# A fused attention and two-layer MoE kernel: the front and the first nine units written out in another order

## The chip, the cores and the metric

One core of one Trainium2 chip runs the whole kernel in one launch. The metric is the device time of a launch in microseconds (us). Engines are named as in the profile: PE (TensorE; PEld its weight loads), DVE (VectorE), ACT (ScalarE), POOL (GpSimd), SP (SyncE, which here only issues DMAs). Each engine runs its instructions in order.

## What is computed

Linear attention with decay over 12 blocks of 64 positions (2 batches, 8 heads, head size 64), then a two-layer MLP on the 1,536 x 512 result, then a second MLP with a softmax gate and a layer norm. Cut to what matters here:

```python
for b in range(12):                                  # blocks of 64 positions, all heads
    intra = einsum('bhic,bhjc->bhij', qb, kb) * Dmask # scores, masked with powers of lam
    intra = einsum('bhij,bhjd->bhid', intra, vb)
    inter = einsum('bhid,bhde->bhie', qb * lam_pow, kv_state)
    out[b] = intra + inter
    kv_state = lam_block * kv_state + einsum('bhsd,bhse->bhde', kb * rev_pow, vb)
h = x @ w_in                                         # 512 -> 2048
x = maximum(0.01 * h, h) @ w_out                     # 2048 -> 512
h = x @ w_in2                                        # 512 -> 1024; then solu, layer norm with g_ln
out = ln(h) @ w_out2                                 # 1024 -> 512
```

## The kernel before

**Attention** is cut into 12 steps, one for each block of 64 positions. A step has four groups of small 64x64 products on PE: scores (`scores_mm`, L196), their product with v (`xs_mm`, L242), the state's increment (`state_mm`, L210) and q times the state (`xq_mm`, L254). Around them stand: the mask on the scores (`scores_ev`, DVE L204), the decay of k (`scale_k`, four ACT instructions of a head pair each, L170), of q (`scale_q`) and of the state (`decay_state`, both on POOL), the new state (`state_ev`, DVE L236) and the split of the result into two float32r words, `x_hi` (ACT L289) and `x_lo` (DVE L293). Steps 0 to 3 stand in front and give the first 512 tokens (block 0); the other eight stand among the units below (`step`, at the units that `step_at` names).

**The first MLP** runs over 3 blocks of 512 tokens and 16 slices of 128 hidden columns: 48 units (b, f). A unit has a first product (`l1_mm`, L422: 12 matmuls 128x512, in three groups of four: hi word of the weight by hi word of x, hi by lo, lo by hi), the leaky ReLU and the split of its result (`l1_split`: ACT L425, ACT L428, DVE L429) and a second product (`l2_mm`, L438: 12 matmuls) which accumulates in four PSUM banks. The loop runs the first product of unit i, then the second one of unit i-1.

**Weights** arrive as int64 pairs of float32 words in pairs of halves: pair n holds w_in slice n ("IN") and w_out slice n-1 ("OUT"), 512 KB each. Unit (0, f) reads pair f's IN half and pair f+1's OUT half. Each half is converted by ACT and DVE in turn: `words` (two ACT passes, L336 over the high word and L337 over the low one), `clamp`, `shift`, `join` (DVE L343, L353, L362), `high` (ACT L392) and `low` (DVE L411). Block 0 needs all of this done unit by unit; later blocks reuse the result.

**What sets the order.** The code is written out by hand, and its last loop ties every instruction of an engine to the one before it, so each engine runs in the order of the code. All loads go through one helper on one queue (SP), which also limits the bytes under way: a load waits for the landing of the load with which it would pass 1.5 MiB.

```python
AHEAD = 3 << 19
    for before, n in reversed(flight):
        ahead += n
        if ahead > AHEAD:
            tc.add_manual_dep(ins, before.name, SYNC, reason="bytes under way")
```

The order of the loads before: tables (132 KB), step 0 (2 x 384 KB of q, k, k and 256 KB of v), pair 0's IN half, step 1, two DMAs of 64 KB that turn the first mask table `dfirst` into `dmask`, steps 2 and 3, pairs 1 to 3, qk and kv of step 4, pair 4, qk of step 5 and so on. kv has one buffer, qk two.

Of the kernel before, what the change touches and what calls it, by code (L numbers as in the profile page):

```python
# [19 lines left out]
NB = 2  # L20
# [4 lines left out]
AHEAD = 3 << 19  # L25
# [19 lines left out]
def fused_kernel(ctx: ExitStack, tc: tile.TileContext, att, vt, tab, cst, w_in, w_out, w_in2, w_out2, out):  # L45
# [23 lines left out]
    dfirst = cp.tile([P, NPAIR, CH], F32, name="dfirst")  # L69
# [18 lines left out]
    def jrows(s, h):  # L88

        return HALF[h] if s < NPRE else HALF[1 - h]  # L90

    def decay(s):

        return dfirst if s < NPRE else dmask

# [17 lines left out]
    def load(queue, out, in_):  # L113

        size = 4
        for n in out.shape:
            size *= n
        ins = queue.dma_start(out=out, in_=in_).ins
        ahead = size
        for before, n in reversed(flight):  # L120
            ahead += n
            if ahead > AHEAD:
                tc.add_manual_dep(ins, before.name, SYNC, reason="bytes under way")
                break
        flight.append((ins, size))

    def load_step(s):

        t = wp.tile([P, 2048], F32, tag="w", name="ldw")
        qkk = t[:, 0:1536].rearrange("p (n c a b) -> p n c a b", n=NB, c=3, a=NPAIR)  # L130
        v = t[:, 1536:2048].rearrange("p (n a b) -> p n a b", n=NB, a=NPAIR)
        for b in range(NB):
            load(act if s + b == 1 and s == 0 else sync, out=qkk[:, b], in_=att[2 * s + b])
        load(sync, out=v, in_=vt[s])
        ld[s] = (qkk[:, :, 0], qkk[:, :, 1], qkk[:, :, 2], v)

# [22 lines left out]
    def scale_q(s, eng):  # L159
# [3 lines left out]
        q = qk_t[s][:, :, 0] if s >= NPRE else ld[s][Q]  # L163
# [3 lines left out]
    def by_pair(out_, in_, factors):  # L167

        for pr in range(NPAIR):
            act.activation(out_[:, :, pr], in_[:, :, pr], AF.Copy, scale=factors[:, pr, CH - 1 : CH])  # L170

    def scale_k(s, eng):
# [3 lines left out]
        kj, last = ld[s][KJ], decay(s)  # L176
        if eng is act:
            by_pair(kj, kj, last)
# [3 lines left out]
    def decay_state(s, eng):  # L182
# [4 lines left out]
        if eng is act:  # L187
            by_pair(sd_t[s], s_t[s], qpow)
        else:
            eng.tensor_tensor(sd_t[s], s_t[s], qpow[:, :, CH - 1 : CH].unsqueeze(1).to_broadcast(SHAPE), op=ALU.mult)  # L190

    def scores_mm(s, bank, b, pr):
        q, k = (qk_t[s][:, :, 0], qk_t[s][:, :, 1]) if s >= NPRE else ld[s][0:2]
        for h in range(2):
            d = rows(h)
            pe.matmul(at(bank, jrows(s, h), b, pr), k[d, b, pr], q[d, b, pr], start=True, stop=True)  # L196

    def scores_ev(s, bank):
# [15 lines left out]
    def state_ev(s, bank):
# [7 lines left out]
        if s not in sd_t:  # L222
            src = bank.rearrange("p (n a b) -> p n a b", n=NB, a=NPAIR)
            for pr in range(NPAIR):
                ins = dve.scalar_tensor_tensor(
# [6 lines left out]
                ).ins  # L232
                added.setdefault(s, ins)
            return
        for src, dst, old in parts(bank, s_t[s + 1], sd_t[s]):
            added[s] = dve.tensor_tensor(dst, src, old, op=ALU.add).ins  # L236

    def xs_mm(s, bank, b, pr):

        for h in range(2):  # L240
            j = jrows(s, h)
# [64 lines left out]
    def load_weights(n, halves=None):  # L306
# [109 lines left out]
    def l1_mm(u, bank):  # L416
# [15 lines left out]
    def l2_mm(u):
        b, f = u
        ghi, glo = gt.pop(u)
        w = wout_t[f].rearrange("p s (m c) -> p s m c", m=KD)
        for s, g, first, last in ((0, ghi, True, False), (1, ghi, False, False), (0, glo, False, True)):
            for m in range(KD):
                pe.matmul(acc[m], w[:, s, m], g, start=(f == 0 and first), stop=(f == NF - 1 and last))  # L438
# [126 lines left out]
    def scan(table, side, first):  # L565

        for pr in range(NPAIR):
# [6 lines left out]
    load(sync, out=tabs, in_=tab)  # L574
    scan(dfirst, 0, None)
    load_step(0)
    load_weights(0)
    load_step(1)
    for h in range(2):
        load(sync, out=dmask[rows(h)], in_=dfirst[HALF[h]])  # L580
    load_step(2)
    load_step(3)
    load_weights(1, IN)
    load_weights(1, OUT)
    load_weights(2)
    load_weights(3)
    load_qk(NPRE)
    load_kv(NPRE)
    load_weights(4)
    load_qk(NPRE + 1)  # L590
    load(sync, out=fix, in_=cst)
    act.mul(nhalf, one, -0.5)


    xb, sb, kb = acc[0:2], acc[2:4], aps[1]
    alone(scores_mm, 0, sb[0])
    scale_k(0, dve)
    scores_ev(0, sb[0])
    scan(qpow, 1, 1.0)
    scale_q(1, pool)  # L600
    words(0)
    both(xs_mm, 0, xb[0], state_mm, 0, kb)
    state_ev(0, kb)
    x_hi(0, xb[0])
    scale_k(1, act)
    decay_state(1, pool)

    alone(scores_mm, 1, sb[1])
    bits(0)
    scores_ev(1, sb[1])  # L610
    x_lo(0, xb[0])
    both(xs_mm, 1, xb[1], state_mm, 1, kb)
    scale_q(2, pool)
    scale_k(2, act)
    alone(scores_mm, 2, sb[0])
    state_ev(1, kb)
    decay_state(2, pool)
    alone(xq_mm, 1, xb[1])
    scores_ev(2, sb[0])
    join(0)  # L620
    x_hi(1, xb[1])
    both(xs_mm, 2, xb[0], state_mm, 2, kb)
    x_lo(1, xb[1])
    scale_q(3, pool)
    scale_k(3, act)
    high(0)

    alone(scores_mm, 3, sb[1])
    state_ev(2, kb)
# [197 lines left out]
```

## Time and profile before

| | us |
|---|---|
| median of 3 runs (448.31 to 450.56) | 448.86 |
| the profiled execution | 449.68 |
| its span on the core | 447.9 |
| PE busy | 434.0 |
| DVE busy | 266.5 |
| ACT busy | 194.9 |
| mean granted PE clock | 0.992 |

The span is what the profiler sees between the first and the last instruction; the execution's own time is 1.8 us longer, and 0.8 us above the median. Busy times are unions of an engine's instructions; a matmul's end is modelled, and its record (390 ns) is longer than its share of the array (227 ns, 12 in 2.72 us), so an idle PE shows a little too small.

### The profile page before, as it was taken

To read this page: it belongs to the slowest core of one execution; us is meant where nothing else is said; L and a number is where in the kernel's file an instruction comes from. 1 tells how busy PE (TensorE), PEld (TensorE's weight loads), DVE (VectorE), ACT (ScalarE), POOL (GpSimd) and SP (SyncE) were. 2 spreads that over 40 slices of the span, in tenths; PEclk is the share of its full clock that TensorE was granted. 3 is DMA by queue.
4 is the path that set the end of the run, shared out by engine and by line. 5 is a ranking of instruction groups with operands and counts; after the bars stand their busy time and mean duration, and the time that the engine had idled before them with its cause. 6 is when DMAs were issued, how large, how long until landed. Compare 5 with 4: busy or idle time off the path is not lost.

```text
span 447.9 us, 7951 instructions
## 1 busy us (share of the span) xinstructions
PE 434.0 (97%) x3252; PEld 358.2 (80%) x3252; DVE 266.5 (60%) x411; ACT 194.9 (44%) x326; POOL 33.0 (7%) x39
## 2 busy tenths in 40 slices
PE   6879899999999999999999999999999999999996
PEld 3868688888788888888888888888888888888886
DVE  3479898998932121211131788817779877777640
ACT  3477977868443232121233678622423322222221
POOL 0502022020102020100000000000000000000000
PEclk9699999999999999999999999999999999999999
DMA  7888875951303030100015653000112322222111
GB/s 264 253 282 265 288 273 153 320 194 50 94 0 97 1 95 1 48 0 1 1 23 184 225 198 122 1 0 5 44 34 58 98 72 74 74 75 74 58 48 47
DMA packets 23859, 46.98 MB, mean 105 GB/s; under 512 B 4368, under 2 KB 12176, under 8 KB 23312
## 3 DMA queue, kind: packets, MB, share of 16 engines
q1 hardware_dynamic: 21952, 44.92, 30.4%
q10 hardware_dynamic: 1872, 1.58, 1.2%
q8 instruction: 25, 0.41, 0.4%
q14 instruction: 10, 0.08, 0.1%
HBM read 37.95 MB, written 3.15 MB: 92 GB/s over the span
## 4 chain that ended last, share of the span: by engine, by line
PE 84%; DMA 8%; ACT 3%; DVE 2%; issue 1%; SPq 1%; ACTq 0%
PE acc L438 25%; PE hps L422 25%; PE acc L550 15%; PE aps L458 6%; PE hps L458 5%; PE acc L458 4%; DMA ldw<-in_att_dram 3%; DMA raww<-in_w_out_dram 2%; PE aps L242 1%; DMA qk<-in_att_dram 1%; PE aps L254 1%; PE acc L560 1%; DMA raww<-in_w_in_dram 1%; DMA kv<-in_vt_dram 1%; ACT x L336 1%; ACT raww L337 1%
## 5 line engine op out<-in xcount | busy, mean ns | idle before, releaser
L422 PE MATMUL hps<-xhi,wio 128*128 128x512 f32 x384 | 102.9, 390 | 3.1 <-ACT wio L392 2.4
L429 DVE TENSOR_TENSOR glo<-hps,ghi 128x512 fp32r<-128x512 f32 x48 | 33.2, 691 | 116.2 <-ACT ghi L428 115.8
L438 PE MATMUL acc<-ghi,wio 128*128 128x512 f32 x384 | 96.2, 393 | 0.1
L422 PEld LDWEIGHTS hps<-xhi,wio 128*128 128x128 f32 x384 | 71.7, 188 | 19.1 <-ACT wio L392 3.4
L438 PEld LDWEIGHTS acc<-ghi,wio 128*128 128x128 f32 x384 | 71.3, 188 | 15.6 <-ACT ghi L428 0.5
L425 ACT ACTIVATE hps<-hps 128x512 f32<-128x512 f32 x48 | 28.0, 583 | 116.6 <-PE hps L422 116.6
L550 PE MATMUL acc<-wb,ln 128*128 128x512 f32 (+1 forms) x312 | 67.6, 373 | 0.0
L550 PEld LDWEIGHTS acc<-wb,ln 128*128 128x128 f32 x312 | 55.3, 188 | 10.2
L422 PE MATMUL hps<-xlo,wio 128*128 128x512 f32 x192 | 51.4, 389 | 0.0
L438 PE MATMUL acc<-glo,wio 128*128 128x512 f32 x192 | 51.3, 389 | 0.0
L422 PEld LDWEIGHTS hps<-xlo,wio 128*128 128x128 f32 x192 | 36.0, 188 | 7.6
L438 PEld LDWEIGHTS acc<-glo,wio 128*128 128x128 f32 x192 | 36.0, 188 | 7.5
L353 DVE SCALAR_TENSOR_TENSOR raww<-x,raww 128x1024 uint32<-128x1024 uint32 (+1 forms) x27 | 31.2, 1154 | 0.5
L336 ACT ACTIVATE x<-raww 128x1024 f32<-128x1024 f32 (+1 forms) x27 | 27.7, 1027 | 7.5 <-DMA raww<-in_w_in_dram 5.2
L362 DVE SCALAR_TENSOR_TENSOR x<-x,raww 128x1024 uint32<-128x1024 uint32 (+1 forms) x27 | 29.6, 1096 | 0.8
L428 ACT CAST ghi<-hps 128x512 fp32r<-128x512 f32 x48 | 28.2, 587 | 1.5
L337 ACT ACTIVATE raww<-raww 128x1024 uint32<-128x1024 uint16 (+1 forms) x27 | 27.9, 1033 | 0.0
L491 POOL TENSOR_TENSOR small<-small,nhalf 128x1 f32<-128x1 f32 x12 | 6.6, 550 | 234.5 <-DVE small L490 234.5
L411 DVE TENSOR_TENSOR wio<-x,wio 128x1024 fp32r<-128x1024 f32 (+1 forms) x20 | 22.2, 1111 | 0.6 <-ACT wio L392 0.5
L553 ACT COPY osb<-acc 128x512 f32<-128x512 f32 (+1 forms) x13 | 7.2, 554 | 32.3 <-PE acc L550 19.2
L165 POOL TENSOR_TENSOR qk<-qk,qpow 128x512 f32<-128x512 f32 x8 | 11.3, 1406 | 135.4 <-PE hps L196 135.4
L458 PE MATMUL aps<-wa,xhi 128*128 128x512 f32 x80 | 19.8, 389 | 0.0
(96 smaller groups left out, 494.6 us busy)
## 6 DMA issues: line engine op xcount, KB each, us to landing
raww<-in_w_out_dram SPq DMA_DIRECT2D x23, 512.0 KB, 4.3
raww<-in_w_in_dram SPq DMA_DIRECT2D x16, 512.0 KB, 5.1
qk<-in_att_dram SPq DMA_DIRECT2D x8, 512.0 KB, 4.1
raww<-in_w_in_dram SPq DMA_DIRECT2D x4, 1024.0 KB, 4.8
lt<-e SPq DMA_DIRECT2D x124, 32.0 KB, 1.8
out_dram<-osb SPq DMA_DIRECT2D x11, 256.0 KB, 2.2
ldw<-in_att_dram SPq DMA_DIRECT2D x7, 384.0 KB, 5.1
kv<-in_att_dram SPq DMA_DIRECT2D x16, 128.0 KB, 3.2
```

The source lines that it names most:

```text
L336: act.activation(x, raw[:, :, 1].bitcast(F32), AF.Copy, scale=HI_SCALE)
L337: act.activation(raw[:, :, 0], raw.bitcast(U16)[:, :, 1], AF.Copy, scale=LO_SCALE)
L353: dve.scalar_tensor_tensor(raw[:, :, 0], x.bitcast(U32), 3, raw[:, :, 0], op0=ALU.logical_shift_left, op1=ALU.bitwise_or)
L362: dve.scalar_tensor_tensor(xu, xu, 0x80000000, raw[:, :, 0], op0=ALU.bitwise_and, op1=ALU.bitwise_or)
L411: dve.tensor_tensor(t[:, 1, halves], x[:, halves], t[:, 0, halves].bitcast(F32), op=ALU.subtract)
L422: pe.matmul(bank, w[:, s, k], x[b][:, k], start=(i == 0), stop=(i == len(terms) - 1))
L425: act.activation(bank, bank, AF.Prelu, alpha=0.01)
L428: act.copy(ghi, bank)
L429: dve.tensor_tensor(glo, bank, ghi.bitcast(F32), op=ALU.subtract)
L438: pe.matmul(acc[m], w[:, s, m], g, start=(f == 0 and first), stop=(f == NF - 1 and last))
L458: pe.matmul(bank, x[b][:, k, o : o + P], w2_t["a", k, half][:, s], start=(i == 0), stop=(i == len(terms) - 1),)
L550: pe.matmul(po[:, 0:n], x[:, k], w2_t["b", k][:, s, cols], start=(i == 0), stop=(i == len(terms) - 1))
```

## The change

- The tables: `dfirst` and its turning by two DMAs are gone. The k and v halves of steps 0 to 3 are loaded turned instead, as for all later steps, in four DMAs of 128 KB (64 partitions each), and q with k in two of 256 KB: six DMAs a step where there were three. Five of step 0's are issued by ACT; the scans that fill the tables (DVE) are listed one head pair at a time.
- The limit of bytes under way is 2 MiB for these loads and for pair 0, 1.5 MiB for all others.
- Pairs 1 to 7 are loaded ahead of step 4's qk and kv.
- PE: scores of steps 0 and 1 stand first; scores of steps 2 and 3 are interleaved with the q products of the step before. Then come the first products of units 0 to 3, then second products; up to unit 8 both are written out in thirds. All is listed by hand, for every engine.
- So that they can be listed apart, `words` is split into `word_hi` and `word_lo` (its two ACT passes), `l1_split` into `leaky`, `g_high` and `g_low`, and the products into `l1_part` and `l2_part` (a third each).
- `step_at`: step 4 moves into unit 7 (written out), steps 5 to 7 to units 10, 12 and 14 (before: 4, 7, 10, 13). From unit 9 on the loop is the old one.

```diff
-AHEAD = 3 << 19
+FIRST, AHEAD = 1 << 21, 3 << 19
...
-    def load(queue, out, in_):
+    def load(queue, out, in_, limit=AHEAD):
...
-            if ahead > AHEAD:
+            if ahead > limit:
...
+    def load_first_qk(s, queues):
+        t = wp.tile([P, 2048], F32, tag="w", name="ldw")
+        qk = qk_t[s] = t[:, 0:1024].rearrange("p (n c a b) -> p n c a b", n=NB, c=2, a=NPAIR)
+        kv = kv_t[s] = t[:, 1024:2048].rearrange("p (c n a b) -> p c n a b", c=2, n=NB, a=NPAIR)
+        for b in range(NB):
+            load(queues[b], out=qk[:, b], in_=att[2 * s + b, :, 0:2], limit=FIRST)
+    def load_first_kv(s, queue=sync):
+        load_turned(s, kv_t[s][:, 0], kv_t[s][:, 1], queue, FIRST)
...
-    step_at = {u: NPRE + j for j, u in enumerate((4, 7, 10, 13, NF + 1, NF + 5, NF + 9, NF + 13))}
+    step_at = {u: NPRE + j for j, u in enumerate((7, 10, 12, 14, NF + 1, NF + 5, NF + 9, NF + 13))}
...
+    both(xq_mm, 1, xb[1], scores_mm, 2, sb[0], (0,))
+    both(xs_mm, 1, xb[1], state_mm, 1, kb, (1,))
...
+    alone(xq_mm, 3, xb[1], (0,))
+    scores_ev(3, sb[1])
+    x_hi(2, xb[0])
+    alone(xq_mm, 3, xb[1], (1,))
+    word_hi(1, OUT)
+    shift(1, IN)
+    both(xs_mm, 3, xb[1], state_mm, 3, kb, (0,))
+    word_hi(2, IN)
+    x_lo(2, xb[0])
+    word_lo(2, IN)
+    clamp(2, IN)
+    word_hi(2, OUT)
+    shift(2, IN)
+    word_lo(2, OUT)
+    both(xs_mm, 3, xb[1], state_mm, 3, kb, (1,))
+    join(2, IN)
+    x_hi(3, xb[1])
...
+    l1_part((0, 0), hps[0], 0)
...
+    l1_part((0, 3), hps[1], 1)
+    join(2, OUT)
+    load_qk(4)
+    word_lo(6)
+    l2_part((0, 0), 0)
...
+    l2_part((0, 0), 2)
+    load(sync, out=fix, in_=cst)
+    shift(4)
+    g_high((0, 2), hps[0])
+    l2_part((0, 1), 0)
...
+    both(xq_mm, 4, aps[0], scores_mm, 5, hps[0], (1,))
+    load_kv(5)
+    state_ev(4, aps[1])
...
+    load_qk(6)
+    low(8)
+    load_weights(12)
```

ACT around the cast of step 3's x (`x_hi`, the CAST into xhi from acc_80) before, in the front; raww and x are a weight half's raw words and its scaled high word:

```order
L392 CAST wio<-x 128x512
L289 CAST xhi_95<-acc_79 128x2x4x64
L336 ACTIVATE x<-raww 128x512
L337 ACTIVATE raww<-raww 128x512
L289 CAST xhi_95<-acc_80 128x2x4x64
```

The same place now (the four L167 are step 3's scale_k):

```order
L167 ACTIVATE ldw<-ldw,dmask 128x2x64 x4
L315 ACTIVATE x<-raww 128x512
L319 ACTIVATE raww<-raww 128x512 x2
L270 CAST xhi_94<-acc_79 128x2x4x64
L315 ACTIVATE x<-raww 128x512 x2
L319 ACTIVATE raww<-raww 128x512
L315 ACTIVATE x<-raww 128x512
L319 ACTIVATE raww<-raww 128x512
L270 CAST xhi_94<-acc_80 128x2x4x64
```

Between the casts of steps 2 and 3 stood two passes over one weight half; now five stand there, the last two over pair 2's OUT half, and three more, of pair 1, stand ahead of step 2's cast.

PE at the first units, before (L422 is the first product, hps its bank; L438 is the second):

```order
L422 MATMUL hps_83<-xhi_95,wio 128x512 x8
L422 MATMUL hps_83<-xlo_98,wio 128x512 x4
L422 MATMUL hps_84<-xhi_95,wio 128x512 x4
L422 MATMUL hps_84<-xlo_98,wio 128x512 x4
L422 MATMUL hps_84<-xhi_95,wio 128x512 x4
L438 MATMUL acc_79<-ghi,wio 128x512
```

and now (L409 and L439 are the same two products):

```order
L409 MATMUL hps_83<-xhi_94,wio 128x512 x8
L409 MATMUL hps_83<-xlo_97,wio 128x512 x4
L409 MATMUL hps_84<-xhi_94,wio 128x512 x4
L409 MATMUL hps_84<-xlo_97,wio 128x512 x4
L409 MATMUL hps_84<-xhi_94,wio 128x512 x4
L409 MATMUL hps_83<-xhi_94,wio 128x512 x4
L409 MATMUL hps_83<-xlo_97,wio 128x512 x4
L409 MATMUL hps_83<-xhi_94,wio 128x512 x4
L409 MATMUL hps_84<-xhi_94,wio 128x512 x4
L409 MATMUL hps_84<-xlo_97,wio 128x512 x4
L439 MATMUL acc_79<-ghi,wio 128x512
```

Two first products stood ahead of the first second one; now four do, the fourth without its last third.

ACT further on, between the first products of units 1 and 4, before (L425 is the leaky ReLU, L428 the cast to ghi, L392 `high`):

```order
L425 ACTIVATE hps_83<-hps_83 128x512
L428 CAST ghi<-hps_83 128x512
L336 ACTIVATE x<-raww 128x1024
L337 ACTIVATE raww<-raww 128x1024
L392 CAST wio<-x 128x512
L336 ACTIVATE x<-raww 128x1024
L337 ACTIVATE raww<-raww 128x1024
L425 ACTIVATE hps_84<-hps_84 128x512
L428 CAST ghi<-hps_84 128x512
L392 CAST wio<-x 128x1024
```

and now (L416, L421, L379 are these three; L315 and L319 the two passes over raw words):

```order
L421 CAST ghi<-hps_84 128x512
L319 ACTIVATE raww<-raww 128x1024
L416 ACTIVATE hps_83<-hps_83 128x512
L379 CAST wio<-x 128x512
L319 ACTIVATE raww<-raww 128x1024
L379 CAST wio<-x 128x512
L315 ACTIVATE x<-raww 128x1024
L416 ACTIVATE hps_84<-hps_84 128x512
L319 ACTIVATE raww<-raww 128x1024
L421 CAST ghi<-hps_83 128x512
L379 CAST wio<-x 128x512
L315 ACTIVATE x<-raww 128x1024
```

The second passes over whole pairs (raww 128x1024, pairs 5, 6 and 7) now stand ahead of the leaky ReLUs, casts and `high` of earlier units.

## Rows read from the trace of the kernel before

**Rows 1.** The page, part 1: busy us (share of the span) x instructions.

```profile
PE 434.0 (97%) x3252; PEld 358.2 (80%) x3252; DVE 266.5 (60%) x411; ACT 194.9 (44%) x326; POOL 33.0 (7%) x39
```

**Rows 2.** Busy time by stretch: from:to, length, busy us (x instructions), clock, DMA share, GB/s.

```profile
5.00:10.00 5.00, 3.49 (x115) 2.72 (x113) 3.25 (x8) 2.14 (x4) 0.00 (x0) 1.00 0.89 299
10.00:15.00 5.00, 2.08 (x52) 1.80 (x52) 1.29 (x2) 1.35 (x5) 2.28 (x2) 0.70 0.90 283
15.00:20.00 5.00, 5.00 (x172) 5.00 (x166) 2.36 (x4) 1.86 (x5) 2.30 (x2) 0.62 0.85 270
20.00:28.00 8.00, 5.31 (x171) 4.81 (x165) 5.39 (x9) 4.69 (x11) 2.29 (x2) 1.00 0.80 256
5.00:30.00 25.00, 17.88 (x494) 15.97 (x493) 13.93 (x25) 11.82 (x27) 6.87 (x6) 0.86 0.85 274
30.00:50.00 20.00, 18.42 (x107) 14.42 (x105) 18.13 (x28) 16.08 (x25) 2.77 (x2) 1.00 0.86 287
45.00:55.00 10.00, 8.08 (x136) 6.37 (x138) 8.37 (x10) 9.20 (x15) 0.00 (x0) 1.00 0.89 311
60.00:70.00 10.00, 10.00 (x46) 8.13 (x45) 9.21 (x10) 8.62 (x14) 0.08 (x1) 1.00 0.95 349
28.00:130.00 102.00, 99.47 (x934) 81.03 (x933) 88.44 (x105) 74.56 (x112) 13.05 (x10) 1.00 0.58 195
```

**Rows 3.** Timeline, 26 to 33 us: start, us, engine, line, instruction [idle before <-releaser].

```profile
26.81 0.59 ACT L289 CAST xhi<-acc 128x512 fp32r<-128x512 f32 x1 [2.65 <-PE acc L254]
...
27.44 2.11 PE L422 MATMUL hps<-xhi,wio 128*128 128x512 f32 x8 [0.68 <-ACT xhi L289]
...
28.50 0.39 SPq L118 DMA_DIRECT2D qk<-in_att_dram  x1
...
30.57 1.37 SPq L118 DMA_DIRECT2D kv<-in_att_dram  x2
```

**Rows 4.** The chain that ended last: start us, us, what.

```profile
41.49 4.61 DMA raww<-in_w_out_dram
46.12 1.17 ACT x L336
...
50.44 3.02 PE hps L422 x12
...
58.44 2.72 PE hps L422 x12
...
207.27 0.93 PE aps L254 x32
```

**Rows 5.** Groups by line and form, 0 to 120 us: xcount | busy us, mean ns | idle before.

```profile
L337 ACT ACTIVATE raww<-raww 128x1024 uint32<-128x1024 uint16 x12 | 13.9, 1161 | 0.0
L336 ACT ACTIVATE x<-raww 128x1024 f32<-128x1024 f32 x12 | 13.8, 1153 | 2.3 <-DVE wio L411 1.5 <-DMA raww<-in_w_out_dram 0.7
L392 ACT CAST wio<-x 128x1024 fp32r<-128x1024 f32 x12 | 12.6, 1051 | 1.0 <-DVE x L362 0.9
...
L428 ACT CAST ghi<-hps 128x512 fp32r<-128x512 f32 x15 | 8.8, 587 | 0.5
L425 ACT ACTIVATE hps<-hps 128x512 f32<-128x512 f32 x15 | 8.8, 585 | 11.9 <-PE hps L422 11.9
...
L170 ACT ACTIVATE kv<-kv,dmask 128x128 f32<-128x128 f32 x16 | 5.1, 391 | 0.0
...
L336 ACT ACTIVATE x<-raww 128x512 f32<-128x512 f32 x7 | 4.7, 671 | 5.2 <-DMA raww<-in_w_in_dram 5.2
L337 ACT ACTIVATE raww<-raww 128x512 uint32<-128x512 uint16 x7 | 4.7, 666 | 0.0
...
L392 ACT CAST wio<-x 128x512 fp32r<-128x512 f32 x7 | 4.3, 618 | 3.3 <-DVE x L362 2.7 <-issue 0.6
...
L289 ACT CAST xhi<-acc 128x512 fp32r<-128x512 f32 x4 | 2.3, 584 | 4.3 <-PE acc L254 4.3
```

More of the change, by code (lines that the diff above doesn't have):

```diff
@@ L564, in fused_kernel, with scan @@
     pool.memset(zero, 0.0)
-    def scan(table, side, first):
-        for pr in range(NPAIR):
+    def scan(table, side, first, pairs=range(NPAIR)):
+        for pr in pairs:
             lam = lams[:, side, pr : pr + 1].to_broadcast([P, CH])
@@ L591, in fused_kernel @@
[L591 to L629, printed above, removed]
-    decay_state(3, pool)
-    alone(xq_mm, 2, xb[0])
-    scores_ev(3, sb[1])
-    both(xs_mm, 3, xb[1], state_mm, 3, kb)
@@ new lines, in fused_kernel @@
+    scale_k(1, act, (2,))
+    scale_k(1, act, (0,))
+    scores_ev(1, sb[1])
+    x_hi(0, xb[0])
+    load_first_kv(3)
+    word_hi(0)
+    x_lo(0, xb[0])
+    state_ev(0, kb)
+    clamp(0)
+    word_lo(0)
+    scale_k(1, act, (1,))
+    shift(0)
+    both(xs_mm, 1, xb[1], state_mm, 1, kb, (0,))
+    join(0)
+    load_weights(1, IN)
+    scale_k(2, act, (0,))
+    scale_k(2, act, (3,))
+    scale_k(2, act, (2,))
+    scale_k(2, act, (1,))
+    load_weights(1, OUT)
+    load_weights(2)
+    load_weights(3)
@@ new lines, in fused_kernel @@
+    both(xs_mm, 3, xb[1], state_mm, 3, kb, (0,))
[9 more added lines that the diff above has]
+    x_hi(3, xb[1])
+    clamp(2, OUT)
+    word_lo(3, IN)
+    join(1, IN)
+    l1_part((0, 0), hps[0], 0)
+    word_hi(3, IN)
+    x_lo(3, xb[1])
+    word_lo(3, OUT)
+    l1_part((0, 0), hps[0], 1)
+    clamp(3, IN)
+    high(1, IN)
+    shift(3, IN)
@@ new lines, in fused_kernel @@
+    l1_part((0, 0), hps[0], 2)
+    high(2, IN)
+    load_weights(5)
+    low(1, IN)
+    word_hi(3, OUT)
+    l1_part((0, 1), hps[1], 0)
+    low(2, IN)
+    leaky(hps[0])
+    g_high((0, 0), hps[0])
+    join(3, IN)
+    l1_part((0, 1), hps[1], 1)
+    load_weights(6)
+    word_lo(4)
+    g_low((0, 0), hps[0])
+    l1_part((0, 1), hps[1], 2)
+    clamp(3, OUT)
+    high(3, IN)
+    l1_part((0, 2), hps[0], 0)
+    clamp(1, OUT)
+    leaky(hps[1])
+    low(3, IN)
+    g_high((0, 1), hps[1])
+    l1_part((0, 2), hps[0], 1)
@@ new lines, in fused_kernel @@
+    leaky(hps[1])
+    word_lo(7)
+    clamp(4)
+    l2_part((0, 0), 2)
[3 more added lines that the diff above has]
+    l2_part((0, 1), 0)
+    load_qk(5)
+    high(3, OUT)
+    join(4)
+    l2_part((0, 1), 1)
+    word_hi(5)
+    l2_part((0, 1), 2)
+    g_low((0, 2), hps[0])
+    scale_k(4, act, (2,))
+    high(4)
+    load_weights(8)
+    clamp(5)
+    l2_part((0, 2), 0)
+    low(3, OUT)
+    g_high((0, 3), hps[1])
+    l1_part((0, 4), hps[0], 0)
+    low(4)
+    scale_k(4, act, (3,))
@@ new lines, in fused_kernel @@
+    word_hi(6)
+    l1_part((0, 4), hps[0], 1)
+    g_low((0, 3), hps[1])
+    word_hi(7)
+    l1_part((0, 4), hps[0], 2)
+    shift(5)
+    l2_part((0, 2), 1)
+    scale_k(4, act, (0,))
+    clamp(7)
+    leaky(hps[0])
+    clamp(6)
+    l2_part((0, 2), 2)
+    scale_k(4, act, (1,))
+    word_lo(8)
+    join(5)
+    l2_part((0, 3), 0)
+    g_high((0, 4), hps[0])
+    shift(6)
+    l2_part((0, 3), 1)
+    high(5)
+    load_weights(9)
+    l2_part((0, 3), 2)
+    g_low((0, 4), hps[0])
+    word_lo(9)
@@ new lines, in fused_kernel @@
+    low(5)
+    l1_part((0, 5), hps[1], 0)
+    l1_part((0, 5), hps[1], 1)
+    join(6)
+    word_hi(8)
+    l1_part((0, 5), hps[1], 2)
+    shift(7)
+    high(6)
+    load_weights(10)
+    l2_part((0, 4), 0)
+    leaky(hps[1])
+    join(7)
+    l1_part((0, 6), hps[0], 0)
+    g_high((0, 5), hps[1])
+    word_lo(10)
+    low(6)
+    l1_part((0, 6), hps[0], 1)
+    high(7)
+    load_weights(11)
+    l2_part((0, 4), 1)
+    g_low((0, 5), hps[1])
+    state_ev(3, kb)
+    word_hi(9)
+    alone(scores_mm, 4, hps[1], (0,))
```

349 lines of the change are left out of this document (203 added, 146 removed).

## The prediction

> **What bounds the kernel now.** I read the page first, then stretches of time, then the rows around the first weight product and the chain of waits. On the page the reader is to see that TensorE (PE) is busy 97% of the span and VectorE 60% [rows 1]: the time can fall only where PE stands still, or where it does work that it need not. The stretches say where that is. From 28 to 130 us PE is busy 99.47 of 102 us, so it stands still 2.53 us in all, most of it between 45 and 55 us [rows 2], and in the chain everything after 120 us is PE. The other idle time lies ahead of the first weight product, which starts at 27.44 us [rows 3]. In 5 to 30 us the loads run at 274 GB/s with the DMA engines 85% busy, in 30 to 50 us at 287 GB/s [rows 2]: the front is paced by loads. The chain says the same: at 41.49 us it goes through the load of a w_out piece, then through ScalarE's two passes over it, before PE goes on at 50.44 us [rows 4].
>
> So two things decide: when the first weight product starts, and how long PE stands still after it. At best the second gives 2.5 us back.
>
> **First product.** It needs x of all four front steps, so it stands behind x_hi(3) on ScalarE (ACT): the cast at 26.81 us and the product at 27.44 us [rows 3]. Before, x_hi(3) waits only for PE. Now it stands on ACT behind both passes over pair 2's w_out half (word_hi and word_lo), and ACT runs in order, so it waits for that load too.
> - When does that load land? Before, 132 KB of tables, 4 x 1,024 KB of steps, 512 KB of pair 0, 128 KB of dmask and 4 x 512 KB of pairs 1 and 2 stand up to it, 6,916 KB. Its landing can be read: with 1.5 MiB allowed under way, the load of qk(4) has to wait for it and is issued at 28.50 us [rows 3]. Now the 128 KB of dmask are gone: 131 KB less at 274 GB/s is 0.5 us, so 28.0 us.
> - Then word_hi 0.67, word_lo 0.67 and x_hi(3) 0.58 us [rows 5]: the product would start at 28.0 + 1.9 + 0.1 = 30.0 us, 2.6 us later than before.
> - The change also lets 2 MiB be under way during the steps' loads. That can at most fill the 15% in which the DMA engines stand idle [rows 2]: 4.6 MB at 274 GB/s are 17 us, of which 15% is 2.5 us. No row shows how much of it a deeper queue fills; between 0 and 2.5 I take 1.0, nearer to none, since the share is 0.86 in 30 to 50 us too, where fewer and larger loads are under way, and 0.95 only at one place [rows 2]. **Term A: +1.6 us.**
>
> **Units 0 to 8.** From pair 1 on the limit is 1.5 MiB as before, so I take 287 GB/s: 512 KiB in 1.83 us. Ten loads stand behind pair 2's, all of pairs 3 to 7, so relative to a first product at 30.0 us, w5's second half lands at 28.0 + 6 x 1.83 = 39.0 and w7's at 46.3 us.
> - PE runs three first products of 2.72 us each [rows 4] and two thirds of a fourth, to 30.0 + 9.97 = 40.0. The second product of unit 0 needs high(1, OUT), which stands on ACT behind word_lo(5): 39.0 + 1.16 + 0.585 (leaky) + 0.62 = 41.4 [rows 5]. PE waits 1.4.
> - Seven thirds of 0.907 us follow, to 47.7. The second product of unit 2 needs high(3, OUT), behind word_lo(7) and g_high: 46.3 + 1.16 + 0.59 + 0.62 = 48.7. PE waits 1.0.
> - One third, to 49.6. The first product of unit 4 needs high(4), behind word_hi(5) 1.15, one scale_k 0.39 and its own 1.05 [rows 5]: 51.3. PE waits 1.7.
>
> That is 4.1 us of waits. Before, the whole stretch from 28 to 130 us had 2.53, about 0.5 of them after 110 us, and I leave those 0.5 in. **Term B: 4.1 + 0.5 - 2.5 = +2.1 us.** If the loads come earlier as in term A, landings and product move together, and the waits stay. If from pair 1 on they come faster, the waits shrink: at the 349 GB/s of 60 to 70 us [rows 2] 512 KiB take 1.5 us, ten loads 3.3 us less, and about 1 us of waits is left.
>
> **Step 4 and later.** The steps of block 1 move from units 4, 7, 10, 13 to 7, 10, 12, 14: the same products, later. The table of kv has one buffer, so load_kv(5) waits on SP for step 4's last product, now in unit 7, and behind it stand load_qk(6) and pairs 12 and 13. Pair 12 is first read in unit 12, four units of 5.4 us on: hidden, price 0, and without that cover a DMA wait of up to 4 us would show at unit 12. The step's own waits (its masked scores on VectorE between conversions) were about 0 before; between 0 and 1 I take 0.4. **Term C: +0.4 us.**
>
> **What costs nothing.** Scores of steps 2 and 3 now run beside the state products of the step before in other quarters of the array; an unpaired group takes 0.93 us [rows 4], so 2 x 0.93 us of PE work goes, but it lies before the first product, where PE is busy 17.9 of 25 us [rows 2] and waits for loads anyway. A step's load goes from three DMAs to six. A pair of 64-partition ones takes SP 1.37 us [rows 3], a whole one 0.39, so a step takes SP about 0.8 + 2.7 = 3.5 us to issue against 3.8 us for its bytes at 274 GB/s: just hidden; uncovered it would cost a part of a microsecond a step. The doubled scans (dmask and qpow, both before the first scores) stand in VectorE's idle front, 13.93 busy of 25 us [rows 2].
>
> **The sum.** 1.6 + 2.1 + 0.4 = +4.1 us on the profiled execution's 449.68 us gives 453.8. That execution is 0.8 us above the median of 448.86 of the runs shown; in their terms I predict **453.0 us**. Within this case: no help from the deeper queue gives +5.1 and both steps' waits 0.6 more, so +5.7 (454.6); full help and C at zero gives 449.68 + 0.1 + 2.1 - 0.8 = 451.1.
>
> **The rivals.**
> - *The other side: the loads come faster.* If pair 2's w_out half lands before about 25.5 us (27.44 less 1.9), x_hi(3) waits for PE alone again. That needs the 6.95 MB at 300 GB/s, and if the rate also nears the 349 GB/s that 60 to 70 us shows, the waits of units 0 to 8 fall to about 0.5: the start 1 us earlier from earlier steps, 2 us of waits gone, so 3 us faster, 445.9. For it: the limit is higher and no load waits any more for VectorE's first table. Against it: 256 to 287 GB/s in the stretches between 15 and 50 us, at an engine share of 0.80 to 0.86 [rows 2].
> - *No change.* The loads gain about as much as the new order asks: first product at 27.5 to 29, waits 2.5 to 3: 448 to 451, say 449.9.
> [...]
>
> That the order is not what is written can be left out: the instructions stand on each engine as listed.
>
> **How the numbers follow.** My forecast, the loads at about the old rate, 0.52; no change 0.24, for my terms are small sums of landings that I may have off by 2 us; faster loads 0.12; lower clock 0.12. A difference of 0.5% (2.2 us) is about what a measurement of this kernel can tell from no change. Slower by more: 0.52 + 0.12 = 0.64; within: 0.24; faster by more: 0.12. The range leaves out most of the fast case and the end of the cold one: 447.0 to 457.0.
>
> **What would show it.** Right: the first weight product at 28 to 30.5 us with ACT's xhi cast just ahead of it and a DMA ahead of that; three waits of PE on wio from ACT between 39 and 52 us; 28 to 130 us with 4 us or more of idle PE. Wrong: a first product before 27.4 us, a rate above 300 GB/s in 5 to 30 us, or no wait for wio in units 0 to 4. [...]

## The result: 0.7% slower

The changed kernel takes 451.6 us (median of 15 runs, 450.13 to 452.67) against 447.95 us for the kernel before beside it (15 runs, 445.71 to 450.94): **ratio 1.0073, 95% interval 1.0053 to 1.0093**: slower, by less than 1%, but the interval is clear of 1. The profiled execution took 450.81 us, 0.8 us less than the median, with a span of 449.0 us.

The page of after, part 1, and below it its stretches, columns as in [rows 2]:

```profile
PE 435.5 (97%) x3252; PEld 358.6 (80%) x3252; DVE 268.2 (60%) x411; ACT 194.3 (43%) x326; POOL 34.5 (8%) x39
```

```profile
5.00:30.00 25.00, 16.77 (x489) 14.24 (x488) 17.23 (x26) 14.56 (x32) 7.79 (x6) 0.79 0.97 300
25.00:30.00 5.00, 2.15 (x45) 1.71 (x38) 4.28 (x8) 4.01 (x7) 0.00 (x0) 0.99 0.94 331
30.00:35.00 5.00, 5.00 (x16) 3.90 (x15) 3.19 (x5) 3.99 (x7) 0.00 (x0) 0.67 0.85 304
30.00:50.00 20.00, 19.39 (x79) 15.50 (x78) 17.11 (x26) 17.76 (x27) 0.00 (x0) 0.92 0.88 301
60.00:70.00 10.00, 10.00 (x71) 8.08 (x71) 9.39 (x11) 7.32 (x10) 2.69 (x2) 1.00 0.10 40
28.00:130.00 102.00, 100.55 (x931) 81.88 (x932) 86.36 (x101) 70.95 (x107) 13.72 (x10) 0.98 0.56 188
110.00:130.00 20.00, 20.00 (x208) 16.55 (x208) 14.61 (x17) 10.87 (x22) 2.35 (x2) 1.00 0.22 72
```

The loads run faster than in [rows 2] (300 instead of 274 GB/s in 5 to 30 us) and PE stands still less behind 28 us (1.45 us instead of 2.53), but just after the first weight products begin the granted clock is 0.67 over 30 to 35 us, so PE ran for part of it at a lower one: 0.50 from 29.90 to 33.31 us, and 1.00 on both sides of that (28.00 to 29.90 and 33.31 to 40.00 us). The timeline of after, ACT and PE around the first product (the counterpart of [rows 3]), and PE's waits further on:

```profile
26.69 0.68 ACT L315 ACTIVATE x<-raww 128x512 f32<-128x512 f32 x1 [0.52 <-DMA raww<-in_w_out_dram]
27.27 0.67 ACT L319 ACTIVATE raww<-raww 128x512 uint32<-128x512 uint16 x1
27.82 0.59 ACT L270 CAST xhi<-acc 128x512 fp32r<-128x512 f32 x1
...
28.46 2.61 PE L409 MATMUL hps<-xhi,wio 128*128 128x512 f32 x8 [2.85 <-ACT xhi L270]
...
48.23 1.20 PE L409 MATMUL hps<-xhi,wio 128*128 128x512 f32 x4 [0.61 <-ACT wio L379]
...
59.77 1.21 PE L409 MATMUL hps<-xhi,wio 128*128 128x512 f32 x4 [0.36 <-ACT wio L379]
```

ACT waits for pair 2's w_out half, runs its two passes, then x_hi(3); PE waits 2.85 us for that and starts at 28.46 us instead of 27.44. Of the three waits forecast behind it, one is there (0.61 us at the first product of unit 4).

**The ledger.** Every trace of this study can be written as: span = start of the first weight product + clock loss + idle PE + rest. Clock loss is (1 - mean granted clock) x length from the first product to 40 us; idle PE is counted from there to 130 us; both come from the stretches of each trace. The two of after, from which its row follows (0.15 x 11.54 = 1.7; 101.54 - 100.55 = 1.0):

```profile
28.46:40.00 11.54, 11.54 (x44) 9.28 (x45) 9.09 (x17) 9.28 (x15) 0.00 (x0) 0.85 0.87 309
28.46:130.00 101.54, 100.55 (x931) 81.88 (x932) 85.90 (x101) 70.49 (x106) 13.72 (x10) 0.98 0.56 188
```

The rest, mostly PE's own work, is what is left over. It is 417.1 to 418.9 us in all 14, so the other three columns tell what an edit did to within about 1.8 us. Ratios are to the kernel before, over all runs; the columns come from one trace each.

| kernel | ratio (95%) | first product | clock loss | idle PE | rest | span |
|---|---|---|---|---|---|---|
| before, the trace shown | 1 | 27.44 | 0.0 | 2.5 | 417.9 | 447.9 |
| before, second trace (b_again) | 1 | 25.71 | 1.7 | 1.9 | 417.5 | 446.8 |
| **after** | 1.0073 (1.0053-1.0093) | 28.46 | 1.7 | 1.0 | 417.8 | 449.0 |
| after, second trace (a_again) | - | 28.79 | 2.8 | 0.4 | 417.1 | 449.1 |
| a_early | 1.0072 (1.0046-1.0099) | 28.61 | 1.7 | 2.0 | 418.3 | 450.6 |
| a_x3 | 1.0060 (1.0036-1.0084) | 26.13 | 0.0 | 4.4 | 418.9 | 449.5 |
| b_late | 1.0053 (1.0028-1.0077) | 28.61 | 3.1 | 1.6 | 417.4 | 450.7 |
| a_units | 1.0024 (1.0003-1.0045) | 25.87 | 0.0 | 3.0 | 418.0 | 446.9 |
| b_units | 1.0056 (1.0033-1.0078) | 25.99 | 1.7 | 4.5 | 418.0 | 450.2 |
| a_fill | 1.0049 (1.0023-1.0075) | 29.39 | 0.0 | 2.4 | 418.7 | 450.4 |
| b_steps_fill | 0.9988 (0.9960-1.0016) | 25.98 | 0.0 | 1.5 | 417.6 | 445.0 |
| a_first15 | 1.0075 (1.0046-1.0104) | 30.42 | 2.1 | 0.9 | 417.7 | 451.1 |
| b_steps | 0.9971 (0.9941-1.0002) | 25.65 | 1.6 | 1.1 | 417.2 | 445.5 |
| b_steps_first | 0.9969 (0.9943-0.9995) | 25.44 | 1.6 | 1.1 | 417.3 | 445.5 |

The traces show only part of the difference. Those of after are 1.1 to 2.3 us longer than those of before, the medians 3.65 us apart: the trace of before that is shown took 1.7 us more than its median, those of after 0.7 and 0.8 us less. a_fill's and a_first15's traces are 1.3 and 1.5 us above their medians.

### The profile page after: what moved, and what is told of

Its sections match the earlier page's. It is cut to its first block, busy times and chain, and to the rows that moved or that the text cites. A ratio compares the mean times of both kernels' runs of the same rounds, so it can differ in the third digit from the quotient of the medians.

```text
span 449.0 us, 7975 instructions
## 1 busy us (share of the span) xinstructions
PE 435.5 (97%) x3252; PEld 358.6 (80%) x3252; DVE 268.2 (60%) x411; ACT 194.3 (43%) x326; POOL 34.5 (8%) x39
## 3 DMA queue, kind: packets, MB, share of 16 engines
q10 hardware_dynamic: 2320, 1.97, 1.5%
## 4 chain that ended last, share of the span: by engine, by line
PE 86%; DMA 12%; ACT 1%; SPq 0%; issue 0%; ACTq 0%
PE acc L439 27%; PE hps L409 26%; PE acc L555 15%; PE aps L463 6%; PE hps L463 5%; DMA raww<-in_w_out_dram 4%; PE acc L463 4%; DMA raww<-in_w_in_dram 3%; DMA ldw<-in_att_dram 2%; PE aps L225 2%; DMA ldw<-in_vt_dram 1%; PE aps L237 1%; DMA qk<-in_att_dram 1%; DMA tabs<-in_tab_dram 1%; PE hps L182 1%; PE aps L196 0%
## 5 line engine op out<-in xcount | busy, mean ns | idle before, releaser
L409 PE MATMUL hps<-xhi,wio 128*128 128x512 f32 x384 | 103.7, 393 | 3.8 <-ACT xhi L270 2.8
L439 PE MATMUL acc<-ghi,wio 128*128 128x512 f32 x384 | 96.5, 392 | 0.0
L409 PEld LDWEIGHTS hps<-xhi,wio 128*128 128x128 f32 x384 | 72.2, 189 | 20.3 <-ACT xhi L270 3.0
L439 PEld LDWEIGHTS acc<-ghi,wio 128*128 128x128 f32 x384 | 71.5, 188 | 15.2
L416 ACT ACTIVATE hps<-hps 128x512 f32<-128x512 f32 x48 | 27.9, 582 | 119.4 <-PE hps L409 119.4
L409 PE MATMUL hps<-xlo,wio 128*128 128x512 f32 x192 | 52.2, 394 | 0.0
L439 PE MATMUL acc<-glo,wio 128*128 128x512 f32 x192 | 51.5, 390 | 0.0
L409 PEld LDWEIGHTS hps<-xlo,wio 128*128 128x128 f32 x192 | 36.6, 191 | 7.8
L439 PEld LDWEIGHTS acc<-glo,wio 128*128 128x128 f32 x192 | 36.0, 188 | 7.5
L315 ACT ACTIVATE x<-raww 128x1024 f32<-128x1024 f32 (+1 forms) x27 | 27.6, 1026 | 4.9 <-DVE wio L398 4.0
L319 ACT ACTIVATE raww<-raww 128x1024 uint32<-128x1024 uint16 (+1 forms) x27 | 27.8, 1033 | 3.6 <-DMA raww<-in_w_out_dram 3.5
L421 ACT CAST ghi<-hps 128x512 fp32r<-128x512 f32 x48 | 28.1, 586 | 1.7 <-PE acc L439 0.4
L398 DVE TENSOR_TENSOR wio<-x,wio 128x1024 fp32r<-128x1024 f32 (+1 forms) x20 | 23.2, 1163 | 2.6 <-ACT wio L379 2.6
```

The lines of the kernel that those rows point to most:

```text
L398: dve.tensor_tensor(t[:, 1, halves], x[:, halves], t[:, 0, halves].bitcast(F32), op=ALU.subtract)
L409: pe.matmul(bank, w[:, s, k], x[b][:, k], start=(part + k == 0), stop=(part == 2 and k == KD - 1))
```

## The experiments

**The kernel before once more (b_again).**

> The kernel before, unchanged, for a second trace of it. If the trace that the prediction rests on is a typical one, the loads run at about 274 GB/s in 5 to 30 us and the first weight product starts within 0.5 us of 27.44. If that execution had slow loads, the rate is over 295 GB/s and the first product starts at 25.5 to 26.5 us, as in b_steps, whose front is the same.

Its stretches and PE's waits:

```profile
5.00:30.00 25.00, 18.94 (x495) 16.28 (x494) 15.84 (x28) 13.55 (x30) 6.85 (x6) 0.86 0.90 299
25.00:30.00 5.00, 4.33 (x13) 3.43 (x13) 4.56 (x8) 4.73 (x9) 0.00 (x0) 0.66 0.92 299
```

```profile
25.71 3.69 PE L422 MATMUL hps<-xhi,wio 128*128 128x512 f32 x8 [0.68 <-ACT xhi L289]
49.40 1.19 PE L422 MATMUL hps<-xhi,wio 128*128 128x512 f32 x4 [1.41 <-ACT wio L392]
```

The trace that the prediction rests on had slow loads: here the rate is 299 GB/s instead of 274, and the first product comes 1.7 us earlier. The same front gave 25.65 us in b_steps.

**The changed kernel once more (a_again).**

> The changed kernel, unchanged, for a second trace of it, as was taken of the kernel before. If its first trace is typical, x_hi(3) again stands behind the landing of pair 2's w_out half, the first weight product starts at 28.0 to 29.5 us with the clock at the lower level for 3.4 us or more after it, and the stretch from there to the end is 420.5 to 421.5 us. If the first trace was an odd one, one of these three is missing.

```profile
25.00:30.00 5.00, 2.36 (x45) 1.98 (x38) 3.64 (x8) 4.08 (x7) 0.00 (x0) 0.50 0.92 315
30.00:35.00 5.00, 5.00 (x15) 3.90 (x14) 2.92 (x5) 2.95 (x6) 0.00 (x0) 0.56 0.92 330
```

```profile
28.79 3.78 PE L409 MATMUL hps<-xhi,wio 128*128 128x512 f32 x8 [2.64 <-ACT xhi L270]
...
48.74 1.07 PE L409 MATMUL hps<-xhi,wio 128*128 128x512 f32 x4
```

All three are there, the last just below its range: the product at 28.79 us behind 2.64 us of waiting for xhi, a mean clock of 0.50 in 25 to 30 us and 0.56 in 30 to 35 us, a stretch of 420.3 us. So the later first product (+2.75 and +3.1 us against b_again) belongs to the change, not to one execution.

**x_hi(3) earlier (a_early, a_x3).** a_early:

```diff
-    word_hi(2, OUT)
     shift(2, IN)
-    word_lo(2, OUT)
...
     x_hi(3, xb[1])
+    word_hi(2, OUT)
+    word_lo(2, OUT)
...
+    high(1, IN)
     word_lo(3, OUT)
...
-    high(1, IN)
```

> The changed kernel with three moves in the order of ScalarE alone: x_hi(3) ahead of both passes over pair 2's w_out half, and high(1, IN) ahead of word_lo(3, OUT), which waits for a load that lands at 30.96 us. Theory Q (the order on ScalarE makes the first product late, term A of the prediction): x_hi(3) waits for TensorE alone, the first product starts at 26.9 us instead of 28.46, the first product of unit 1 at about 30 us instead of 32.57, and 1.5 to 2.4 us of the time go: about 449.6. Theory L (the loads pace units 0 to 6): the first product is as early, but TensorE then waits 1.5 to 2.4 us more for wio between 40 and 60 us, where ScalarE waits for loads that land at 39.97 and 56.45 us; the time moves by less than 0.6 us.

Neither: the first product was no earlier (28.61 us), so this run could not tell the two apart. The order was only half mended. In its timeline ACT now stood at `word_hi` of pair 2's IN half, 1.75 us, and x_hi(3) behind that:

```profile
26.86 0.66 ACT L315 ACTIVATE x<-raww 128x512 f32<-128x512 f32 x1 [1.75 <-DMA raww<-in_w_in_dram]
27.42 0.66 ACT L319 ACTIVATE raww<-raww 128x512 uint32<-128x512 uint16 x1
27.98 0.57 ACT L270 CAST xhi<-acc 128x512 fp32r<-128x512 f32 x1
```

a_x3 moves it ahead of all of pair 2 (and on DVE `join(1, IN)` and x_lo(3) ahead of pair 2's clamp):

```diff
+    x_hi(3, xb[1])
+    high(1, IN)
+    x_lo(3, xb[1])
     word_hi(2, IN)
...
     word_lo(2, IN)
```

> The changed kernel with x_hi(3) ahead of all four passes over pair 2 on ScalarE, high(1, IN) right behind it, and on VectorE join(1, IN) and x_lo(3) ahead of the clamp of pair 2, so that no load stands between the last state products of the front and the first weight product. Theory Q (term A: the passes over pair 2 ahead of x_hi(3) hold up the first product, and in a_early the half of them that was left still did): the first product starts 0.6 to 1.0 us after the last product of the front, at 26.2 to 27.7 us against 28.5 to 30.4 in the changed kernel's variants so far; the stretch from there to the end was 420.4 to 422.0 us in all six traces, so the time falls by 1.5 to 2.5 us, to about 449.6. Theory L (the loads pace units 0 to 8): the product is as early, but the stretch behind it grows to 422.5 us or more by waits for wio, and the time stays within 0.6 us of 451.6.

The first product came 2.3 us earlier, as both theories said, at a granted clock of 1.00 (26.13 to 40 us); the time did not follow (1.0060 against 1.0073). The ledger shows why: clock loss and late start went, 4.0 us in all, and 3.4 us of new idle PE and 1.1 us of rest came. PE's waits in a_x3:

```profile
31.84 1.20 PE L409 MATMUL hps<-xhi,wio 128*128 128x512 f32 x4 [0.84 <-DVE wio L398]
34.16 1.20 PE L409 MATMUL hps<-xhi,wio 128*128 128x512 f32 x4 [1.13 <-DVE glo L426]
39.53 1.19 PE L439 MATMUL acc<-ghi,wio 128*128 128x512 f32 x4 [0.49 <-ACT wio L379]
48.51 1.20 PE L409 MATMUL hps<-xhi,wio 128*128 128x512 f32 x4 [1.41 <-ACT wio L379]
60.22 1.19 PE L409 MATMUL hps<-xhi,wio 128*128 128x512 f32 x4 [0.52 <-ACT wio L379]
```

The last of them is the instruction that started at 59.77 us in after: 2.3 us of head start were used up by 60 us. Unit 4 shows it at one place. Its first product, with the same work of PE ahead of it, starts at 48.23 and 48.74 us in the two traces of after, at 48.51 here and at 48.59 in b_units below, while the very first product stands at 28.46, 28.79, 26.13 and 25.99 us. (In a_early, a_fill and a_first15, whose traces had later loads, unit 4 starts at 49.66 to 50.30 us.) Theory L holds so far, that units 0 to 6 can't use an earlier start; whether the loads or the order of the units is to blame was open.

**x_hi(3) late in the kernel before (b_late).**

```diff
     words(1, IN)
+    bits(1, IN)
+    words(1, OUT)
+    words(2, IN)
+    words(2, OUT)
     x_hi(3, xb[1])
-    bits(1, IN)
     x_lo(3, xb[1])
-    words(1, OUT)
...
-    words(2, IN)
...
-    words(2, OUT)
```

> The kernel before with one edit, the part of the change that term A prices: on ScalarE x_hi(3) stands behind both passes over pair 1's w_out half and all passes over pair 2. Theory Q: the first product waits for the load of pair 2's w_out half, which landed at 25.2 and 28.5 us in the two traces of this front, and two passes, so it starts at 27.1 to 30.4 us instead of 25.7 to 27.4; with an unchanged stretch behind it the time rises by 1.5 to 2.9 us, to about 450.7. Theory L: the first product is later, but the weights of units 0 to 4 are then ready ahead of it and waits for wio (2.4 us in the trace of before) vanish, so the time stays within 0.6 us of 448.5.

```profile
28.61 1.65 PE L422 MATMUL hps<-xhi,wio 128*128 128x512 f32 x3 [3.05 <-ACT xhi L289]
```

```profile
30.00:35.00 5.00, 5.00 (x14) 3.91 (x13) 3.83 (x7) 1.98 (x4) 0.00 (x0) 0.53 1.01 316
```

Theory Q: the product at 28.61 us, ratio 1.0053. Idle PE fell only to 1.6 us, and the wait ahead of the product (3.05 us) was followed by a mean clock of 0.53 in 30 to 35 us, 3.1 us of loss. So this edit alone makes the kernel before slower by 0.5% (0.3 to 0.8), against 0.7% for the whole change. Its price holds both the later start and the lower clock behind it; this run does not part them.

**Half of the change each (a_units, b_units).** a_units keeps a_x3's front and takes before's units (`l1_mm((0, 0))`, `l1_mm((0, 1))`, then the old loop with first and second products in turn) with before's loads behind pair 3; b_units is the reverse. Both have the later steps.

> Half of the change, first half: the front of a_x3 (the changed kernel's, with x_hi(3) early), but from the first weight product on the units in the order of the kernel before (first and second products taken in turn, a pair's passes all together), with its loads behind pair 3, and the later steps. In a_x3 the first product started 2.3 us earlier than in the changed kernel and the stretch behind it grew from 420.6 to 423.4 us. Theory U (the new order of units 0 to 8 can't use an earlier start: VectorE and ScalarE have the halves of the weights ready too late for four first products in a row): with before's units the stretch behind the first product is 420 to 421 us, as in the three traces of before's order; first product at 26 to 27 us, span 446 to 448 us, time about 448.5, like the kernel before. Theory F (the front leaves the conversions behind, whatever comes next): the stretch stays at 423 us and the time at 451.

> Half of the change, second half: the front of the kernel before up to the first weight product (its limit of 1.5 MiB too), then the passes over pair 2 and the changed kernel's order of units 0 to 8, its loads and its later steps. Theory U: the first product starts at 25.5 to 26.5 us as in before, but the stretch behind it is 422.5 us or more, with two to four waits of TensorE for VectorE and ScalarE between 30 and 61 us, and the time is about 450.5 to 451.5, as in a_x3. Theory F (the changed front is what costs): the stretch is 420 to 421 us and the time is 448.5 or less.

Theory U is the nearer one twice. With before's units the changed front gives a stretch of 421.0 us and 1.0024; with the new units before's front gives 424.2 us and 1.0056. The halves differ by 0.32%, give or take 0.31%, so the ratios only just part them. Nor is the changed front free: a_units has the later steps, which alone measured 0.9971 (b_steps, below), and against that it is 0.5% slower, give or take 0.4%. In its trace ACT's casts of weights wait 3.8 us for DVE from 24 to 40 us, in b_steps 1.8, and idle PE is 3.0 us instead of 1.1. That is theory F in part, and what of the changed front does it was not tested. The waits of b_units begin with the longest, at unit 2, and ACT and DVE show what it stood behind:

```profile
28.86 1.07 PE L428 MATMUL hps<-xhi,wio 128*128 128x512 f32 x4
...
30.68 1.07 PE L428 MATMUL hps<-xhi,wio 128*128 128x512 f32 x4
34.83 2.08 PE L428 MATMUL hps<-xhi,wio 128*128 128x512 f32 x4 [3.09 <-DVE glo L445]
...
48.59 1.19 PE L428 MATMUL hps<-xhi,wio 128*128 128x512 f32 x4 [0.34 <-ACT wio L398]
```

```profile
31.74 0.63 ACT L398 CAST wio<-x 128x512 fp32r<-128x512 f32 x1
32.25 0.70 ACT L334 ACTIVATE x<-raww 128x512 f32<-128x512 f32 x1
32.81 0.62 ACT L435 ACTIVATE hps<-hps 128x512 f32<-128x512 f32 x1
33.47 0.59 ACT L440 CAST ghi<-hps 128x512 fp32r<-128x512 f32 x1
```

```profile
30.00:35.00 5.00, 1.91 (x9) 1.30 (x8) 4.09 (x8) 4.97 (x10) 0.00 (x0) 0.94 0.89 293
```

Unit 2's first product needs unit 0's bank. Unit 0's product was done when unit 1's began, at 28.86 us, but its leaky ReLU (L435) ran at 32.81, behind passes over weights on an ACT that was busy 4.97 of 5 us, and DVE's glo (the low word of the unit's result, which DVE takes from the same bank) came after that. In a_units the next in line is unit 0's second product, which needs ghi alone; it waited too, but 1.77 us, and later PE waited 1.12 us more, once:

```profile
33.42 2.11 PE L439 MATMUL acc<-ghi,wio 128*128 128x512 f32 x8 [1.77 <-ACT ghi L421]
49.80 1.21 PE L409 MATMUL hps<-xhi,wio 128*128 128x512 f32 x4 [1.12 <-ACT wio L379]
```

**The clock (a_fill, b_steps_fill).** Both write 12 products of constants into the idle bank of unit 1, b_steps_fill in four places of the front of b_steps, a_fill in one:

```diff
     both(xs_mm, 3, xb[1], state_mm, 3, kb, (1,))
+    fill(12, hps[1])
```

> The changed kernel with 12 bf16 products of 128x512 on constants, into the bank of unit 1, written on TensorE right behind the last state products of step 3, where it now stands still for 2.85 us before the first weight product at 28.46 us. They keep TensorE busy and change no result. Theory C (the clock): the 3.41 us at half clock from 29.90 us come from that stillness and cost 1.7 us; with the fill the clock stays at 1.00 from 23 us on, the first product still starts at 28.3 to 28.8 us, and the time falls by 1.2 to 1.7 us, from 451.6 to about 450.2. Theory L (the loads pace units 0 to 6): the clock stays up as well, but the gain comes back as waits of TensorE for wio behind ScalarE up to 60 us; idle time in 28 to 130 us grows from 1.45 to about 3 us and the time moves by less than 0.6 us. If the clock falls all the same, theory C is wrong about its cause, and the time stays at 451.6.

> The kernel before with the steps of block 1 in units 7, 10, 12, 14 and with 12 bf16 products on constants in four places of the front where TensorE waits (3 ahead of the products with the state of steps 1 and 2, 4 ahead of those of step 3, 2 ahead of the first weight product). In b_steps the clock was at 0.5 from 25.46 to 28.87 us, just when the first weight products ran. Theory C: the clock stays at 1.00 there, and up to 1.7 us go, from 448.1 to about 446.8. Theory L: the clock stays up, but waits for wio take the gain back: within 0.6 us of 448.1. Slower than that if the fillers hold up the front's own products (12 of 0.21 to 0.43 us).

```profile
27.17 2.57 PE L581 MATMUL hps<-const-bfloat16-1.0 128*128 128x512 bf16 x11 [0.16 <-issue]
```

```profile
29.39:40.00 10.61, 10.61 (x48) 8.63 (x47) 8.85 (x16) 9.01 (x15) 0.00 (x0) 1.00 0.89 314
```

In both traces the clock stayed at 1.00 from the first weight product on, while after, a_again and b_steps, the same orders without the fill, lost 1.6 to 2.8 us. With work for PE in its waits neither trace lost any; without such work, that of before that is shown did not either (1.00 from 27.44 to 40 us). What the higher clock is worth is less clear. 1.0049 against 1.0073 points to 1.1 us, just below theory C's range and above theory L's; b_steps_fill against b_steps points to nothing, as theory L has it; and the intervals overlap. In a_fill idle PE rose from 1.0 to 2.4 us, which is theory L's part, but in that execution the first product came later too (29.39 us, where 28.3 to 28.8 was expected). All runs together say more: the mean granted clock of the span is 0.993 over 88 executions of the kernel before, 0.985 over 15 of after and 0.991 over 12 of a_fill. (That mean counts the front ahead of the first product too.) With nearly the clock of before, a_fill is still 0.5% slower than it, so the clock alone is not the difference.

**The limit of bytes under way (a_first15, b_steps_first).**

```diff
-FIRST, AHEAD = 1 << 21, 3 << 19
+FIRST, AHEAD = 3 << 19, 3 << 19
```

That is a_first15, the changed kernel with 1.5 MiB for all loads. b_steps_first is the opposite: b_steps with 2 MiB for the loads of the front.

> The changed kernel with the limit of 1.5 MiB under way for the front loads too (FIRST equal to AHEAD). The prediction gave the 2 MiB limit 1.0 us of the first product. By that, the rate in 5 to 30 us falls from 300 to about 285 GB/s, pair 2's w_out half lands at about 27.7 us instead of 26.67, the first product starts at about 29.5 us and the time rises by about 1 us, to 452.6. If the limit does nothing (the rise to 300 GB/s comes from the new order of loads), landings and time stay within 0.4 us.

> b_steps with the limit of 2 MiB under way for the steps' loads and pair 0, the part of the change that the prediction gave 1.0 us. In before's order of units an earlier first product should count in full, so by the prediction the first product starts at about 25 us instead of 25.65 to 26.0 and the time falls by 0.7 to 1.0 us from 448.1 to about 447.3. If the queue is deep enough at 1.5 MiB (as a_first15 against the changed kernel suggests), the time is within 0.5 us of 448.1.

Neither time moved: 1.0075 against 1.0073, 0.9969 against 0.9971. In a_first15's trace the rate fell to 281 GB/s and the first product came at 30.42 us, as by the prediction, but one trace against two is little where the same front differs by 1.7 us between executions. The difference of two such ratios is uncertain by 0.35 to 0.4%, so up to about 1.6 us could hide in it: the 1.0 us of the prediction is neither seen nor ruled out.

**The later steps alone (b_steps).** `step_at` with 7, 10, 12, 14 in the kernel before.

> The kernel before with one part of the change alone: the steps of block 1 in units 7, 10, 12, 14 instead of 4, 7, 10, 13. Term C of the prediction gave the later steps +0.4 us (a step's own waits). By that the time is 448.0 to 448.6 against a median of 447.95 before. Rival: the later steps are what made the changed kernel slower, through VectorE and ScalarE work that meets the weight conversions of pairs 9 to 13 and through SP, which stands behind load_kv(5): +2 us or more, 450 or above. Other rival: the later step 4 leaves the early units free of its 64-row products and of its loads, which speeds the conversions: 447 or below.

0.9971 (0.9941 to 1.0002): not slower, and rather faster; its trace has 1.1 us of idle PE against 1.9 and 2.5 in the traces of before. With the 2 MiB limit as well (b_steps_first, 447.52 us) it is just faster than before beyond its interval, and the best version found.

## Why the prediction was right, and where not

The sign, the range and the place of the first loss were right: 453.0 us forecast, 451.6 measured. That the sum came so near is in part luck. Of the prediction's three signs of being right one came, the first product at 28.46 us behind the cast and a load; instead of three waits for wio between 39 and 52 us there is one, and instead of 4 us or more of idle PE there are 1.45. And the lower clock, to which it gave 0.12, is there: 0.67 over 30 to 35 us.

- **Term A** had the right mechanism (x_hi(3) behind the load and two passes) and was sized against an odd execution. The load landed at 26.7 us, where the prediction, with its 1.0 us for the 2 MiB limit, had 27.0, and the two passes and the cast took 1.8 us, not 2.0: +1.0 us against [rows 3] instead of +1.6. Against the second trace of before it is +2.75 us. b_late shows the term by itself, with the lower clock that comes with it. Whether the loads came sooner by the limit, by their new order or by chance is not shown.
- **Term B** is the step that failed: "landings and product move together, and the waits stay". Idle PE behind the product is 1.0 and 0.4 us, not 4.6. The prediction had the late product in its sum; what it had wrong is that the loads behind pair 2 came quicker, which it names only as an if, and that PE itself was slower, which it has only as a case of 0.12. Unit 4 shows both, counted from the landing of pair 2's w_out half (28.0 us in the working, 26.7 in after). By the working its weights are ready 51.3 - 28.0 = 23.3 us behind that landing, and PE, had it not waited, would be there 4.1 us sooner. In after they were ready at 48.23 - 26.7 = 21.5 us, 1.8 us sooner. Of the rest most went as slow products: the 11 groups of four matmuls ahead of unit 0's second product took 40.21 - 28.46 = 11.75 us, not 9.97, which is the clock loss. What was left is the wait at 48.23 us. The loads, by the chain of after: the second half of pair 6, eight 512 KiB loads behind pair 2's landing at 26.7 us, landed at 34.93 + 5.04 = 39.97; 13.3 us, not 8 x 1.83 = 14.6.

```profile
24.92 6.04 DMA raww<-in_w_out_dram
30.97 3.94 DMA raww<-in_w_in_dram
34.93 5.04 DMA raww<-in_w_out_dram
```

  The waits are real where the product is early and the clock high: a_x3 (26.13 us, 1.00) has them at the second product of unit 0 (0.49 us) and at unit 4 (1.41), two of the three places named, and 1.97 us more at units 1 and 2, where the prediction looked for none. So A and B look like two prices of which PE pays about one: b_late pays A alone (1.0053), b_units B with the later steps (1.0056), and the whole change, which has both, measured 1.0073 (at most 1.0093), where the product of the two would be 1.011. Their intervals are too wide to show that by the times; the idle PE of the ledger and the start of unit 4 are the better witnesses.
- **Term C** was +0.4; alone it measured 0.9971, to 1.0002 at most.
- **The lower clock** had a chance of 0.12; it is in both traces of after (1.7 and 2.8 us). But it is in the second trace of before as well (1.7 us), so against that trace it explains 0 to 1.1 us, and part of it stands in place of the waits of term B. a_fill's ratio points to 1.1 us too. The cold end of the range, up to 457.0 us, no run shows: the longest run of after took 452.67 us, that of all kernels here 454.01. Nor does the wait ahead of the first product alone tell when the clock falls. In a_again the clock was at 0.50 in 25 to 30 us, behind a wait of 2.64 us; in after, behind 2.85 us, it was at 1.00 until 29.90 us and fell behind the product's start; behind 0.68 us it was at 0.66 in 25 to 30 us in b_again and at 1.00 in the trace of before that is shown.
- **What was to cost nothing** cost nothing: the loads stood still in 60 to 70 us (40 GB/s), behind load_kv(5), and PE was busy 10.00 of 10 us there and 20.00 of 20 us from 110 to 130 us. That two interleaved groups take PE no longer than one is in the trace of before: of `xs_mm` and `state_mm` 28 products each start from 22.28 to 23.10 us, so 32 of each in 0.94 us, and an unpaired group of 32 took 0.93.

What stays open: how much of the difference is the clock's, what in the changed front costs a_units its time, what the 2 MiB limit is worth below about 1.6 us, and the part of the 3.65 us that the traces do not show.

## What to carry to other kernels

When a change makes one thing late and asks for another earlier, don't add the two prices: ask which of them the engine would still pay if the other were mended, and test by mending one. An engine that runs in order should not have a pass over a load ahead of the instruction that releases the long stretch of work; but mending that gains only what the next wait leaves: a_x3's first product came 2.3 us earlier and its time did not move (1.0060 against 1.0073). And take a second trace of the kernel before: here two executions of it differed by 1.7 us in the very stretch that the change was priced in.

## What was not expected

- The same front's loads ran at 274, 299 and 313 GB/s (5 to 30 us) in three executions (before, b_again, b_steps), with the first product at 27.44, 25.71 and 25.65 us.
- Clock loss and idle PE seem to trade against each other: while PE ran at a granted clock of 0.50, weights got ready. a_again lost 2.8 us to the clock, after 1.7; idle PE was 0.4 and 1.0 us, and the spans were 449.1 and 449.0 us.
